# FFT filter and gated feed-forward on one core: an early table, an inverse in natural order, turns by halves

## The chip, the cores and the metric

The kernel runs on one core of one Trainium2 chip. Times are microseconds (us) of the device for one execution. The engines are PE (matmuls; its weight loads are listed apart as PEld), DVE, ACT and POOL (elementwise work), and SP, which here only issues transfers. Each has its own queue and works it off in order; they wait for each other by semaphores. The time before is the median of three runs: 863.05 us (862.38 to 863.38).

## The reference: what is computed

Eight batches of 3008 rows by 256 columns are filtered along the rows in the frequency domain, and every row of the result goes through a gated feed-forward:

```python
X = np.fft.rfft(x, axis=1)
Y = X * (filt_r + 1j * filt_i)[None]
y = np.fft.irfft(Y, n=x.shape[1], axis=1)          # (8, 3008, 256)
t = y.reshape(8 * 3008, 256)
gate = np.maximum(t @ w_gate, 0.0)                 # 256 -> 1536
out = (gate * (t @ w_val)) @ w_out                 # 1536 -> 256
```

Inputs and output are float32. All 24064 rows of the output are written.

## The kernel before

3008 is 94 times 32, so the transform is done in two steps, of 94 points over n1 and of 32 points over n2, each as matmuls with tables of cosines and sines. d is the column index, 0 to 255. For one batch the stages are these.

- Stage A (`a_bank`, L272, and for part of batch 1 `a_halves`, L329): matmul of rows of x with a table, `WA` or `WH`, results in PSUM tiles psA. ACT copies them to bfloat16.
- A turn: a transpose in blocks of 32 by 32 on DVE, which brings n2 to the partitions.
- The 32-point step (`fwd`, L442), the product with the filter (`product`, L459 to L462), the inverse 32-point step (`inv`, L485) into PSUM tiles psD. ACT and DVE copy these out (L498 for batch 0).
- Another turn, for batch 0 `turn_d`, from the tile AS0 (seen as `DS0`) to the tile dCb (seen as `D0`). Later batches go through a scratch area in HBM instead.
- Stage C (`item_c`, L605): matmul with `M1` for some columns n2 and one half h of d, into psY. ACT or DVE copies it to `yT`, in which d lies on the partitions (L613).
- Feed-forward: `gv` (L622: psV and psG; L625: ACT copies psV; L627: DVE makes prod) and `o_part` (L643, psO), in 47 blocks of 512 rows, 12 steps each.

The program has no scheduler: each engine gets its instructions in the order in which the Python code runs. The work of batches 1 to 7 up to stage C is placed among the feed-forward steps by hand (`at_step`). Ahead of the first feed-forward step stands a prologue: batch 0 from load to its first stage C, and much of batch 1's stage A. Its tiles come from a pool `pro`, which is closed at the end, so that the feed-forward's tiles take its place.

The end of the prologue goes like this. SP's queue loads batch 1's x: two quarters of the first half tile, six transfers of `load_halves` (rows n1 and n1 + 47 side by side), the last quarters, and then the table WH. `first_b` runs batch 0's 32-point steps with items of batch 1's stage A between (`item`). POOL adds and subtracts the two halves (`fold_halves`, L318 and L319). Then come, in this order, `turn_d` for both h (DVE), three items (PE), `a_halves` for both h (PE; needs WH and POOL's results), two items, stage C of batch 0's first two items, two more items, the first turn of batch 1, and on POOL a change of sign in every second row of the filter's imaginary part, `Fti` (L743). `conj` is a bfloat16 part of the tile `tabs`; `conj32` is its float32 copy, used in the prologue.

`y_items(0)` is 2: the first stage C has an item of five columns n2 and one of a single column, for each h. That makes twelve matmuls, each with a weight load of 128 by 128 from dCb.

In the kernel before, batch 0's inverse is laid down in pairs: `DS0` and `D0` are seen as (k, c, f) with c = 0 to 127, and f = 0 to 3 holding two columns n2 and, within each, the two halves h of d side by side. A turn moves 4-byte words, each the two halves of one (n2, c); the innermost two words of its access pattern lie side by side. `turn_d(h)` then covers the columns c of one half of c, and both halves h of d in each.

Of the kernel before, what the change touches and what calls it, by code (L numbers as in the profile page):

```python
# [12 lines left out]
FP32 = mybir.dt.float32  # L13
BF16 = mybir.dt.bfloat16
ALU = mybir.AluOpType
# [20 lines left out]
def _ap(t, offset_elems, ap_list):  # L36
    return dataclasses.replace(
        t, offset=t.offset + offset_elems, ap=[list(p) for p in ap_list]
    )
# [77 lines left out]
def kernel(  # L117
# [10 lines left out]
    nc = tc.nc  # L128
    B, S_, D = x.shape
# [11 lines left out]
    wh_h = np.zeros_like(wa_h)  # L141
# [5 lines left out]
    consts = ctx.enter_context(tc.tile_pool(name="consts", bufs=1))  # L147
# [5 lines left out]
    def bank(name, *shape):  # L153

        i = free.pop(0)
        t = ps.tile([128, *shape], FP32, tag=f"bank{i}", bufs=1, name=name)
        held[id(t)] = i, t
        return t

    def done(t):  # L160
        free.append(held.pop(id(t))[0])

    prologue = ExitStack()
    pro = prologue.enter_context(tc.tile_pool(name="pro", bufs=1))
# [6 lines left out]
    WA = pro.tile([128, 128], FP32)  # L171
    WH = pro.tile([128, 128], FP32)
    AS0 = pro.tile([128, 4, N2 // 2, D // 8, 4], BF16)
    DS0 = AS0.rearrange("p q n c f -> p (q n c f)").rearrange("p (k c f) -> p k c f", c=D // 2, f=4)
    dCb = consts.tile([128, 48, D], BF16)
    D0 = dCb[:, 0:32, :].rearrange("p n d -> p (n d)").rearrange("p (k c f) -> p k c f", c=D // 2, f=4)
    AS1 = [dCb[:, 32:48, :].rearrange("p n d -> p (n d)").rearrange("p (l c d) -> p l c d", l=NC2, d=D // 2)]
    WF = consts.tile([128, 4, 32], FP32)
    M1 = consts.tile([128, 2, N1], BF16)
# [4 lines left out]
    Fti = consts.tile([128, NG // 2, D], BF16)  # L184
# [7 lines left out]
    def load_x(b, engs, cols, ms=range(3)):  # L192
        w = NX2 * D
        for c, c0, c1 in cols:
            for m in ms:
                rows = min(32, B * N1 - (b * N1 + 32 * m))
                engs[m % len(engs)].dma_start(XF[c][m:m + 4 * rows - 3:4, c0:c1],  # L197
                              _ap(x, (b * N1 + 32 * m) * N2 * D + c * w + c0,
                                  [[N2 * D, rows], [1, c1 - c0]]))
# [2 lines left out]
    H = NG // 2  # L202
    FILT = ((filt_r, Ftr), (filt_i, Fti))
    tabs = pro.tile([128, tab_h.shape[1]], BF16, tag="tabs", bufs=1)
    conj32 = pro.tile([128, 2], FP32, tag="conj32", bufs=1)
    perm, conj, own = tabs[:, 0:64], tabs[:, 64:66], tabs[96:, 66:578]

    def make_back_t(r):
# [97 lines left out]
    def load_halves(b):  # L306

        for m in range(3):
            for s in range(2):
                r = 64 * s + m  # L310
                nc.sync.dma_start(halves[r:r + 61:4].rearrange("p k n d -> p k (n d)"),
                                  _ap(x, ((b * N1 + 16 * m) * N2 + NC2 * P_HALF + 4 * s) * D,
                                      [[N2 * D, 16], [N1 // 2 * N2 * D, 2], [1, 4 * D]]))
# [25 lines left out]
    def turn_pairs(dst, src):  # L339

        nc.vector.transpose(dst.bitcast(FP32).rearrange("p k c g -> p c k g"),
                            src.bitcast(FP32).rearrange("p n c g -> p c n g"))
# [5 lines left out]
    def turn_1(i):  # L348
        w = D // 8
        src = AS1[1 + i // 2].rearrange("p l c d -> p (l c) d")  # L350
        turn_a(ats[1][:, 1, :, i * w:i * w + w], src[:, :, i % 2 * w:i % 2 * w + w])
# [4 lines left out]

    def turn_d(h):

        e = slice(h * D // 4, h * D // 4 + D // 4)
        turn_pairs(D0[:, :, e], DS0[:, :, e])  # L360

    def store_half(b):
        w = N2 * D // 2
# [4 lines left out]
    def load_half(b):  # L368
        w = N2 * D // 2
        for q in range(4):  # L370
            nc.sync.dma_start(ats[b][32 * q:32 * q + 32, 0, 0:NG, :],
                              _ap(Abuf[b], q * NG * w, [[D // 2, 32], [w, NG], [1, D // 2]]))
# [102 lines left out]
    def inv(b, q):  # L475

        psD = [bank("psD", 2, D) for c in range(4)]
        last = 0 if b else 1
        for m in range(2):
            for k in range(last + 1):  # L480
                for r in range(2):
                    for c in range(4):
                        for e in range(2):
                            i = 2 * q + m
                            nc.tensor.matmul(psD[c][64 * e:64 * e + 64, m],  # L485
                                             (I2t, I2u)[k][32 * c:32 * c + 32, r, 2 * i + e, :],
                                             tus[b, i, e, k][32 * c:32 * c + 32, r],
                                             start=(k == r == 0), stop=(k == last and r == 1),
                                             tile_position=(32 * c, 64 * e))
        dst = sb.tile([128, 8, D], BF16, tag="dsb", bufs=3, name="dsb") if b else DS0  # L490
        def out(cs):
            for c in cs:
                copy = nc.vector.tensor_copy if (c % 2 if b else (q, c) in ((1, 2), (1, 3), (2, 0), (2, 1))) else nc.scalar.copy
                if b:
                    copy(dst[:, c:8:4, :], psD[c])
                else:
                    k, g = 4 * q + c // 2, c % 2 * 2
                    copy(dst[:, k:k + 3:2, :, g:g + 2], psD[c].rearrange("p m (f e) -> p m e f", f=2))  # L498
                done(psD[c])
        if not b:  # L500
            return out(range(4))

        def rest():
            out((2, 3))
            for z in range(4):
                nc.sync.dma_start(_ap(Dbuf[b], (64 * (z // 2) + z % 2) * NG * D + 8 * q * D,
                                      [[2 * NG * D, 32], [1, 8 * D]]),
                                  dst[32 * z:32 * z + 32])
        out((0, 1))
        return rest  # L510

# [38 lines left out]
    def d_rows(b, n2, h):  # L550

        if b:
            return dCs[b, n2 // 8][:, n2 % 8, h * 128:(h + 1) * 128]
        return D0[:, n2 // 2, :, n2 % 2 * 2 + h]

    def load_d(b):

# [34 lines left out]
    def y_items(k):  # L592

        n = 0
        while n < len(Y_COLS) and (Y_COLS[n][0] * N2 + Y_COLS[n][1]) * N1 < (k + 1) * W:
            n += 1
        return n

    def item_c(m, h):

        b, n2, c = Y_COLS[m]
        psY = bank("psY", c * N1)
        t = (b * N2 + n2) * N1
        for o, _, col, n1, w in runs(t, c * N1):
            nc.tensor.matmul(psY[:, o:o + w], d_rows(b, col, h),  # L605
                             M1[:, 1, n1:n1 + w] if b == 0 else M1[:NROW, 0, n1:n1 + w],
                             start=True, stop=True)
        o = 0
        while o < c * N1:
            p = (t + o) % NYT  # L610
            w = min(c * N1 - o, NYT - p)
            copy = nc.vector.tensor_copy if h and m < y_items(0) else nc.scalar.copy
            copy(yT[:, h, p:p + w], psY[:, o:o + w])  # L613
            o += w
        done(psY)
# [63 lines left out]
    q = NX2 * D // 4  # L679
# [32 lines left out]
    nc.sync.dma_start(hold, Ftr[0:2, 4, 0:8])  # L712
    load_x(1, sp, ((0, 0, 2 * q), (0, 2 * q, 4 * q)))
    load_halves(1)
    load_x(1, sp, ((1, 2 * q, 4 * q),))
    nc.sync.dma_start(WH, nc.inline_tensor(wh_h, name="dft_wh").ap())
    items = iter([(p, s, h) for p in (0, 1, 3) for h in range(2) for s in range(2)])

    def item(n):
# [9 lines left out]
    for h in range(2):  # L729
        turn_d(h)  # L730
# [4 lines left out]
    new_at(1)  # L735
    store_half(1)
    load_half(1)
    for m in range(y_items(0)):
        for h in range(2):
            item_c(m, h)  # L740
    item(2)
    turn_1(0)
    nc.gpsimd.tensor_scalar(Fti, Fti, conj[:, 0:1], 1.0, op0=ALU.mult, op1=ALU.mult)  # L743
    nc.sync.dma_start(WF, nc.inline_tensor(fold_h, name="dft_fold").ap())
    prologue.close()
    fs = ctx.enter_context(tc.tile_pool(name="fs", bufs=2))
# [87 lines left out]
```

## Time and profile before

| what | value |
|---|---|
| median of three runs | 863.05 us |
| the profiled execution, its own time | 863.78 us |
| its span, first to last instruction | 861.7 us |
| instructions | 20276 |
| PE busy | 845.9 us, 98% of the span |
| DVE busy | 578.5 us, 67% |
| ACT busy | 498.8 us, 58% |
| POOL busy | 462.0 us, 54% |
| mean granted TensorE clock | 0.999 |
| DMA | 101.66 MB, mean 118 GB/s |

A line of a group names source line, engine, operation, tiles (out <- in) and shape, then the count, after the bar the busy time and the mean of one in ns, and after the second bar how long the engine was idle just before and what ended that. A line of the order of time gives start, length, engine, source line, operation, tiles and count; instructions that follow each other are merged, so the length is that of the merged run. The chain is followed back from the last instruction: at each step to what released it, or to the instruction before it on its engine. Matmuls overlap in the array, so a start tells more than a length.

### The profile page before, as it was taken

To read this page: it belongs to the slowest core of one execution; us is meant where nothing else is said; L and a number is where in the kernel's file an instruction comes from. 1 tells how busy PE (TensorE), PEld (TensorE's weight loads), DVE (VectorE), ACT (ScalarE), POOL (GpSimd) and SP (SyncE) were. 2 spreads that over 40 slices of the span, in tenths; PEclk is the share of its full clock that TensorE was granted. 3 is DMA by queue.
4 is the path that set the end of the run, shared out by engine and by line. 5 is a ranking of instruction groups with operands and counts; after the bars stand their busy time and mean duration, and the time that the engine had idled before them with its cause. 6 is when DMAs were issued, how large, how long until landed. Compare 5 with 4: busy or idle time off the path is not lost.

```text
span 861.7 us, 20276 instructions
## 1 busy us (share of the span) xinstructions
PE 845.9 (98%) x7505; PEld 497.0 (58%) x7622; DVE 578.5 (67%) x865; ACT 498.8 (58%) x943; POOL 462.0 (54%) x496
## 2 busy tenths in 40 slices
PE   8899999999999999999999999999999999999998
PEld 4456655655555565655556565566655665666665
DVE  3878865777557776577765777658766578655553
ACT  5766565556655565555665565655566555565553
POOL 6847890488977765866757766767550032100001
PEclk9999999999999999999999999999999999999999
DMA  9995375333872339633295333853455222511112
GB/s 239 221 186 132 100 153 147 103 112 103 196 194 80 77 95 182 181 87 97 78 212 156 99 97 92 194 155 80 100 116 124 97 61 52 128 38 32 37 32 56
DMA packets 103150, 101.66 MB, mean 118 GB/s; under 512 B 21767, under 2 KB 90151, under 8 KB 102379
## 3 DMA queue, kind: packets, MB, share of 16 engines
q1 hardware_dynamic: 83695, 77.99, 34.6%
q0 software_dynamic: 18848, 21.68, 12.2%
q8 instruction: 60, 0.98, 0.5%
q10 hardware_dynamic: 508, 0.68, 0.3%
q14 instruction: 39, 0.32, 0.1%
HBM read 58.30 MB, written 45.88 MB: 121 GB/s over the span
## 4 chain that ended last, share of the span: by engine, by line
PE 92%; DMA 2%; DVE 2%; ACT 1%; SPq 1%; issue 1%
PE psG L622 29%; PE psO L643 28%; PE psV L622 25%; PE psF L408 3%; PE psY L605 2%; DVE prod L627 2%; PE psA L272 2%; ACT vsb L625 1%; PE psD L485 1%; DMA XF<-in_x_dram 1%; PE psX L442 1%; SPq L197 1%; DMA WH<-dft_wh 1%; DVE tt L462 0%; PE psA L329 0%
## 5 line engine op out<-in xcount | busy, mean ns | idle before, releaser
L627 DVE SCALAR_TENSOR_TENSOR prod<-psG,vsb 128x512 bf16<-128x512 f32 x564 | 389.0, 690 | 234.5 <-ACT vsb L625 229.6
L625 ACT CAST vsb<-psV 128x512 bf16<-128x512 f32 x564 | 331.9, 588 | 218.0 <-DVE prod L627 130.1
L622 PE MATMUL psG<-yT,WgT 128*128 128x512 bf16 x1118 | 333.1, 379 | 5.6
L643 PE MATMUL psO<-WoT,prod 128*128 128x256 bf16 x2256 | 336.5, 273 | 0.4
L622 PE MATMUL psV<-yT,WvT 128*128 128x512 bf16 x1023 | 313.6, 380 | 0.1
L643 PEld LDWEIGHTS <-prod 128*128 128x128 bf16 x2256 | 220.7, 98 | 143.4
L622 PEld LDWEIGHTS <-WgT 128*128 128x128 bf16 x1128 | 110.0, 98 | 133.8 <-issue 1.0
L472 POOL TENSOR_TENSOR pp<-tt,uu 128x256 bf16<-128x256 f32 x84 | 60.9, 725 | 170.5 <-DVE uu L462 160.6
L622 PEld LDWEIGHTS <-WvT 128*128 128x128 bf16 x1128 | 100.4, 98 | 36.9 <-issue 25.6
L613 ACT CAST yT<-psY 128x470 bf16<-128x470 f32 (+16 forms) x134 | 58.7, 456 | 46.8 <-PE psY L605 46.6
L652 ACT COPY osb<-psO 128x512 f32<-128x512 f32 x92 | 53.8, 585 | 25.3 <-PE psO L643 23.9
L665 POOL DMA_DIRECT2D out_dram<-osb x5 | 2.6, 535 | 119.2 <-ACT osb L652 117.7
L462 DVE TENSOR_TENSOR tt<-psX,Ftr 128x512 f32<-128x512 f32 (+1 forms) x93 | 63.3, 682 | 0.5 <-PE psX L442 0.5
L462 DVE TENSOR_TENSOR uu<-psX,Fti 128x512 f32<-128x512 f32 (+1 forms) x93 | 63.1, 680 | 0.6 <-DMA Fti<-in_filt_i_dram 0.6
L473 POOL TENSOR_TENSOR pp<-tt,uu 128x256 bf16<-128x256 f32 x84 | 60.9, 725 | 0.0
L394 POOL TENSOR_TENSOR fold<-XF 128x1024 f32<-128x1024 f32 x24 | 56.4, 2348 | 7.7 <-DMA XF<-in_x_dram 7.2
L395 POOL TENSOR_TENSOR XF<-XF 128x1024 f32<-128x1024 f32 x24 | 56.4, 2352 | 1.9
L381 POOL DMA_DIRECT2D XF<-in_x_dram x76 | 45.5, 601 | 2.0 <-issue 0.8
L264 POOL CAST scr<-prod 128x8 f32<-128x8 bf16 x19 | 3.6, 190 | 77.9 <-DVE prod L627 68.8
L415 DVE CAST asb<-psF 128x512 bf16<-128x512 f32 x48 | 30.9, 685 | 17.8 <-PE psF L408 17.8
L415 ACT CAST asb<-psF 128x512 bf16<-128x512 f32 x48 | 25.8, 589 | 28.9 <-PE psF L408 28.9
L605 PE MATMUL psY<-M,dCb 96*128 96x94 bf16 (+2 forms) x514 | 39.9, 205 | 0.0
(74 smaller groups left out, 460.7 us busy)
## 6 DMA issues: line engine op xcount, KB each, us to landing
Dbuf<-dsb SPq DMA_DIRECT2D x84, 128.0 KB
dCb<-Dbuf SPq DMA_DIRECT2D x56, 192.0 KB
XF<-in_x_dram POOLq DMA_DIRECT2D x38, 256.0 KB, 6.9
Abuf<-asb SPq DMA_DIRECT2D x96, 96.0 KB
at<-Abuf SPq DMA_DIRECT2D x18, 512.0 KB
XF<-in_x_dram POOLq DMA_DIRECT2D x76, 96.0 KB, 5.3
XF<-in_x_dram SPq DMA_DIRECT2D x28, 256.0 KB
out_dram<-osb SPq DMA_DIRECT2D x69, 94.0 KB
```

The lines of the kernel that those rows point to most:

```text
L394: tt(t, xp[:, 0:2], xp[:, 2:4], op=ALU.add)
L395: tt(xp[:, 2:4], xp[:, 0:2], xp[:, 2:4], op=ALU.subtract)
L415: copy(asf[:, :, q, :], banks[q])
L462: nc.vector.tensor_tensor(p, psX, filt, op=ALU.mult)
L472: nc.gpsimd.tensor_tensor(p[:, 0], tt[:, 0], uu[:, 1], op=ALU.subtract)
L473: nc.gpsimd.tensor_tensor(p[:, 1], tt[:, 1], uu[:, 0], op=ALU.add)
L605: nc.tensor.matmul(psY[:, o:o + w], d_rows(b, col, h), M1[:, 1, n1:n1 + w] if b == 0 else M1[:NROW, 0, n1:n1 + w], start=True, stop=True)
L613: copy(yT[:, h, p:p + w], psY[:, o:o + w])
L622: nc.tensor.matmul(pt[:, :W], w[:, h, ft * 128:(ft + 1) * 128], yT[:, h, y0:y0 + W], start=(h == 0), stop=(h == 1))
L625: nc.scalar.copy(vsb, psV[:, :W])
L627: nc.vector.scalar_tensor_tensor(prod, in0=psG[:, :W], scalar=0.0, in1=vsb, op0=ALU.max, op1=ALU.mult)
L643: nc.tensor.matmul(psO[:, t % 2], prods[ft][:, t * 128:(t + 1) * 128], WoT[:, ft, :], start=(ft == 0), stop=(ft == NFT - 1))
```

## The change

Three things are changed; the matmuls, their number and the order of the stages stay.

- The load of WH is issued on SP's queue after the six transfers of the halves and ahead of the last three transfers of x.
- Batch 0's inverse is laid down as rows of 256 columns d, one row for each n2. The copies out of psD write whole rows; `turn_d(h)` takes the columns of one half h of d, for all 32 rows, as 4-byte words of two neighbouring columns; the weight loads of batch 0's stage C read 128 neighbouring elements. The first stage C is done for the first half of d and then for the second.
- `conj32` lives in the pool that is not closed, and the change of sign of Fti takes its factor from there.

```diff
-    DS0 = AS0.rearrange("p q n c f -> p (q n c f)").rearrange("p (k c f) -> p k c f", c=D // 2, f=4)
+    DS0 = AS0.rearrange("p q n c f -> p (q n c f)").rearrange("p (j d) -> p j d", d=D)
     dCb = consts.tile([128, 48, D], BF16)
-    D0 = dCb[:, 0:32, :].rearrange("p n d -> p (n d)").rearrange("p (k c f) -> p k c f", c=D // 2, f=4)
+    D0 = dCb[:, 0:32, :]
...
-    conj32 = pro.tile([128, 2], FP32, tag="conj32", bufs=1)
+    conj32 = consts.tile([128, 2], FP32)
...
     def turn_d(h):
 
-        e = slice(h * D // 4, h * D // 4 + D // 4)
-        turn_pairs(D0[:, :, e], DS0[:, :, e])
+        dst, src = (t[:, :, h * D // 2:(h + 1) * D // 2].bitcast(FP32).rearrange("p n c -> p c n") for t in (D0, DS0))
+        nc.vector.transpose(dst, src)
...
-                    k, g = 4 * q + c // 2, c % 2 * 2
-                    copy(dst[:, k:k + 3:2, :, g:g + 2], psD[c].rearrange("p m (f e) -> p m e f", f=2))
+                    copy(dst[:, 8 * q + c:8 * q + c + 5:4, :], psD[c])
...
-        return D0[:, n2 // 2, :, n2 % 2 * 2 + h]
+        return D0[:, n2, h * 128:(h + 1) * 128]
...
     load_halves(1)
+    nc.sync.dma_start(WH, nc.inline_tensor(wh_h, name="dft_wh").ap())
     load_x(1, sp, ((1, 2 * q, 4 * q),))
-    nc.sync.dma_start(WH, nc.inline_tensor(wh_h, name="dft_wh").ap())
...
-    for m in range(y_items(0)):
-        for h in range(2):
+    for h in range(2):
+        for m in range(y_items(0)):
             item_c(m, h)
     item(2)
     turn_1(0)
-    nc.gpsimd.tensor_scalar(Fti, Fti, conj[:, 0:1], 1.0, op0=ALU.mult, op1=ALU.mult)
+    nc.gpsimd.tensor_scalar(Fti, Fti, conj32[:, 0:1], 1.0, op0=ALU.mult, op1=ALU.mult)
```

## The prediction

> **What bounds the kernel now.** I read the page's busy times first, then the chain that ended last, then that chain between 25 and 50 us, then the order of time of DVE, PE and POOL around 40 us, and last the groups kept apart by shape.
>
> ```profile
> PE 845.9 (98%) x7505; PEld 497.0 (58%) x7622; DVE 578.5 (67%) x865; ACT 498.8 (58%) x943; POOL 462.0 (54%) x496
> PE 92%; DMA 2%; DVE 2%; ACT 1%; SPq 1%; issue 1%
> ```
>
> PE carries the chain nearly all the time. After about 46.5 us, where the feed-forward matmuls (L622, L643) begin, the change touches nothing that PE waits for, so whatever it moves up to there is passed on to the end one for one. The chain there:
>
> ```profile
> 32.65 7.40 DMA WH<-dft_wh
> 40.05 0.14 issue
> 40.18 2.26 PE psA L329 x16
> 42.44 1.91 PE psA L272 x4
> 44.35 0.52 PE psY L605 x12
> 44.87 1.78 PE psA L272 x4
> 46.66 0.43 PE psV L622 x2
> ```
>
> PE waits for the table WH until 40.05 us. From there it runs without a gap: the matmuls of the halves, two items of batch 1, batch 0's first stage C (psY, twelve matmuls), two more items, feed-forward. The turns are not in this chain; they lie beside it:
>
> ```profile
> 35.98 2.84 PE L272 MATMUL psA<-XF,WA 128*128 128x512 f32 x6
> 36.29 2.37 POOL L319 TENSOR_TENSOR XF<-XF 128x1024 f32<-128x1024 f32 x1
> 37.47 4.70 DVE L341 STREAM_TRANSPOSE dCb<-AS 128x2048 f32<-128x2048 f32 x2
> 40.18 0.65 PE L329 MATMUL psA<-sum,WH 64*64 64x512 f32 x2 [1.35 <-DMA WH<-dft_wh]
> 44.19 0.68 PE L605 MATMUL psY<-M,dCb 128*128 128x94 bf16 x12
> ```
>
> DVE ends the two turns at 42.17 us and PE begins to read their result at 44.19: they have 2.0 us to spare. What one costs depends on its access pattern, and the kernel has both kinds:
>
> ```profile
> L341 DVE STREAM_TRANSPOSE dCb<-AS 128x2048 f32<-128x2048 f32 x2 | 4.7, 2383 | 0.1
> L341 DVE STREAM_TRANSPOSE at<-AS 128x1024 f32<-128x1024 f32 x4 | 4.7, 1225 | 13.1 <-ACT AS L284 13.1
> L336 DVE STREAM_TRANSPOSE at<-asb 128x512 f32<-128x512 f32 x4 | 4.3, 1082 | 1.5 <-ACT asb L296 1.5
> ```
>
> L341 walks pairs: two 4-byte words side by side, then a jump. It takes 2383/2048 = 1.16 and 1225/1024 = 1.20 ns per word. L336 walks single words, each a jump of 128 bytes on the reading side and 256 on the writing side from the last: 1082/512 = 2.11 ns per word, nearly twice as long.
>
> **The change part by part.**
>
> *Table of the halves.* WH goes on SP's queue ahead of the last three loads of x instead of behind them. SP is free to issue it at 30.22 us instead of 32.65; even with the same 7.40 us to landing that is 37.6, and with the queue in order it lands shortly after the halves, which POOL had at 33.87. PE ends the six matmuls before it at 38.82, and POOL's difference (L319), the third matmul's other need, ends at 38.66. So the wait of 1.35 us goes whole: PE would reach stage C at 44.35 - 1.35 = 43.0. The three loads that WH passes are issued one issue (0.6 us) later; their bytes and WH's are all in by about the 40.05 of before, and their first reader comes after the halves' 2.26 us, at about 41.1. Price nothing, 1 us of cover, and more below.
>
> *Natural order of d: copies out of psD.* The twelve copies (eight on ACT at 594 ns, four on DVE at 682) write rows without a break instead of pairs. The copies of the later batches write so from the same kind of bank: 593 on ACT, 685 on DVE. Zero.
>
> *Natural order: the turns.* Still two instructions of 2048 words, but their access pattern now takes the same 4-byte column of 32 rows, single words 512 bytes apart on both sides. That is L336's kind. The lower end of the unknown price is L341's 2.35 each (nothing here turns faster). From L336: its successor starts 0.98 us after it, so 4 x 0.98 = 3.92 as a step; with its whole duration, 4 x 1.08 = 4.32. The strides are longer than L336's, and if that doubled the price once more it would be 8.6, the upper end, for which no row speaks. I take 4.2 each, between the two readings of the nearest row and toward the dearer one. DVE starts them at 37.47 as before, since the copies cost the same: first done at 41.7, second at 45.9.
>
> The SBUF — State Buffer page of the Trainium skill (Specifications) says that SBUF has 16-byte lines and needs at least two accesses per line for full bandwidth. By that rule the new pattern loses what the pairs had, and the two rows above agree with it; a rule of one word per cycle whatever the stride would leave the turns at 2.35 and make the sum the first rival's below.
>
> *Stage C by halves of d.* The loop now does both items of the first half, then both of the second, so that the first half needs only the first turn. In the built order of the changed kernel, however, only the very first weight load waits for the first turn's count; the second weight load, still of the first half, already waits for the count of the second turn. Rows of the two halves interleave in one tile, so the waits do not tell them apart. PE is in order: one of the twelve matmuls can run at 43.0, eleven stand behind the second turn, and behind them the last two items and the whole feed-forward.
>
> So: second turn 45.87; first matmul after a wait 0.13 later (as after WH: 40.05 to 40.18), 46.0; eleven of the twelve, 11/12 x 0.52 = 0.48, to about 46.5, after which the next psA starts. Before, the first psY started at 44.19 and the next psA 0.52 later, 44.71. In starts: 46.0 + 0.48 = 46.5 against 44.71, **+1.8 us**. With 3.92 per turn the same sum gives +1.3, with 4.32 +2.1. The 1.35 us that WH saves is inside this: PE only waits longer, and without it nothing would be slower yet.
>
> What stands behind: DVE's copies of the second half into yT (0.81) come right after the matmuls and are covered by the 1.78 of psA, as before; the first turn of batch 1's at follows 1.8 later, and so does its reader, since PE is late as well. SP's store of the half for batch 1 waits for ACT copies ahead of stage C, which come earlier: no harm.
>
> *Weight loads of stage C.* Batch 0's 64 loads read rows without a break instead of every fourth element: 113 ns before, 98 in the later batches. They lie beside matmuls, whose starts are 0.52/12 = 43 ns apart in spite of 113-ns loads. Zero; the bound below is 64 x 15 ns = 1.0 us, which I do not expect.
>
> *Fti's signs.* The factor comes from a 4-byte copy that outlives the prologue. One POOL instruction, 2.86 us before (42.01 to 44.87), and POOL then idles 9.1 us; its reader comes at 63.7. Even at twice the time, nothing.
>
> **Against the runs shown.** The profiled execution took 863.78 with a span of 861.7, so 2.1 lies around the span; it is 0.7 above the median 863.05. The sum is made within the span and put on the median: 863.05 + 1.8 = 864.9, or 0.21%. A measurement of this kernel can tell about 0.2%, 1.7 us, from no change, so this sits at the border.
>
> **The rivals.**
>
> *The turns keep their pace (other side).* If single words cost what pairs do, the second turn ends at 42.17, ahead of PE's 43.0, and WH's gain stands: 863.05 - 1.35 = 861.7. It decides wherever both turns together take under 5.5 us. For: same opcode, same number of words. Against: L336. A turn that gains only partly lands between 861.7 and 864.
>
> *The granted clock falls in the gap.* PE would stand still from about 43.1 to 46.0, 2.9 us. The longest wait before is 1.35 us, and the granted clock stayed 1.00 there. But at the end of the run it does fall:
>
> ```profile
> 856.00:858.00 2.00, 1.90 (x18) 1.46 (x15) 0.49 (x2) 0.00 (x0) 1.76 (x4) 1.00 0.57 153
> 860.00:860.50 0.50, 0.00 (x0) 0.00 (x0) 0.00 (x0) 0.00 (x0) 0.00 (x0) 1.00 0.41 90
> 860.50:861.00 0.50, 0.00 (x0) 0.00 (x0) 0.00 (x0) 0.00 (x0) 0.00 (x0) 0.58 0.00 0
> 861.00:861.70 0.70, 0.00 (x0) 0.00 (x0) 0.00 (x0) 0.00 (x0) 0.00 (x0) 0.50 0.00 0
> ```
>
> (Busy time by stretch; the third value from the right is the granted clock.) It goes from 1.00 to 0.50 at about 860.6, 2.7 us after the last matmul's end at 857.9. A gap of 2.9 could meet that in some executions. PE at half speed for a time as long as the gap loses half of it, 1.5 us, twice that if two such times pass: 866.4 to 867.9. The page TensorE: Matmul & The Clock Gate of the Trainium skill (Part 1) gives a free-running window of about 3.4 us; by that page a gap of 2.9 would seldom fill one, and one window at half speed would cost 1.7.
>
> *The longer strides double the price again.* 8.6 per turn: second turn at 54.7, PE 8.8 us later than in the forecast: 873.7. Only the length of the strides speaks for it.
>
> **How the numbers follow.** The forecast's case, turns at L336's pace and no fall of the clock, 0.66: its own range is 864.0 to 865.4, and 0.36 of it lies over the 0.2% bound of 864.8, 0.30 under it. The clock falls: 0.17. Strides dearer still: 0.05. Turns at their old pace or partly: 0.12, of which 0.03 is faster by over 0.2% (weight loads or noise on top), 0.09 within. Slower 0.36 + 0.17 + 0.05 = 0.58, within 0.30 + 0.09 = 0.39, faster 0.03. The range reaches down a little below the forecast's own, 863.4, for partly slower turns, and up to 868.2, the end of the clock's case with some noise; the old pace and the doubled stride are left out.
>
> **What would show it.** The transposes of dCb at some 4.2 us each, ending near 46; PE waiting for WH no more, its halves from 38.9; one psY matmul near 43.1, then PE idle 2.4 to 3 us with the transpose of dCb as the releaser, eleven more from 46; everything later by 1.3 to 2.1. Wrong if the transposes take 2.4 us each, if the second psY matmul runs ahead of the second turn, or if the granted clock between 46 and 50 us is not 1.00.

## The result and the profile after

| | before | changed |
|---|---|---|
| median | 862.86 us (862.10 to 864.76, 6 runs) | 866.84 us (865.44 to 867.15, 6 runs) |
| profiled execution, its own time | 863.78 | 866.74 |
| its span | 861.7 | 864.6 |
| start of the feed-forward (first psV) | 46.49 | 49.45 |
| from there to the start of the last matmul | 811.14 | 811.11 |

The changed kernel is slower: ratio 1.0041, interval 1.0028 to 1.0054. (One of the executions further below, 1482.28 us long at a mean granted clock of 0.556, is left out of its kernel's figures.) The last two rows say where: all 2.96 us between the two profiled executions arise ahead of 49.45 us, and nothing is gained or lost behind it.

The page of the changed kernel, its busy times and the shares of the chain that ended last:

```profile
PE 847.4 (98%) x7505; PEld 496.8 (57%) x7622; DVE 582.1 (67%) x865; ACT 498.9 (58%) x943; POOL 462.1 (53%) x496
...
PE 92%; DVE 3%; ACT 2%; issue 1%; DMA 1%; SPq 0%; DVEq 0%
```

DVE is busy 3.6 us longer, and the chain that ended last now runs through it. The same chain from 37 us on (start, length, what):

```profile
37.33 8.34 DVE dCb L360 x2
45.71 1.04 PE psY L604 x11
46.76 2.85 PE psA L272 x4
```

The transfer of WH, which stood here before, is gone; the two turns stand in its place. In order of time (start, length, engine, line, operation, tiles, shape, count, idle time before it):

```profile
37.33 8.32 DVE L360 STREAM_TRANSPOSE dCb<-AS 128x2048 f32<-128x2048 f32 x2
...
38.62 0.65 PE L329 MATMUL psA<-sum,WH 64*64 64x512 f32 x2
...
42.32 0.20 PE L604 MATMUL psY<-M,dCb 128*128 128x94 bf16 x1
...
45.71 1.04 PE L604 MATMUL psY<-M,dCb 128*128 128x94 bf16 x11 [3.19 <-DVE dCb L360]
...
46.55 3.06 PE L272 MATMUL psA<-XF,WA 128*128 128x512 f32 x4
...
49.45 0.59 PE L621 MATMUL psV<-yT,WvT 128*128 128x512 bf16 x2
```

The halves start without a wait. PE does one psY matmul and then stands still for 3.19 us, until the second turn ends. The group of the turns (busy us, mean ns of one):

```profile
L360 DVE STREAM_TRANSPOSE dCb<-AS 128x2048 f32<-128x2048 f32 x2 | 8.3, 4220 | 0.1
```

4220/2048 = 2.06 ns per word. After the gap something more is lost: eleven psY that started every 43 ns before now take 0.84 us until the next psA starts, and the four psA that took 1.78 us from start to start take 49.45 - 46.55 = 2.90. The busy times by stretch give the reason (us; busy PE, PEld, DVE, ACT, POOL; granted clock; DMA share; GB/s):

```profile
44.00:46.00 2.00, 0.29 (x4) 0.29 (x5) 1.66 (x1) 0.00 (x0) 0.11 (x1) 0.84 1.10 162
46.00:48.00 2.00, 2.00 (x12) 1.36 (x10) 0.81 (x2) 0.69 (x2) 0.00 (x0) 0.50 1.31 245
48.00:50.00 2.00, 2.00 (x5) 0.73 (x5) 0.00 (x0) 1.00 (x4) 0.00 (x0) 0.80 1.07 310
```

The granted clock is 0.50 from 45.37 to 48.78 us by its records, 3.413 us, just as PE takes up work again. So the 2.96 us between the profiled executions are: eleven psY at 45.71 and, at full clock, the next psA at 45.71 + 0.48 = 46.19 against 44.71 before, +1.48; and half speed, (0.84 - 0.48) + (2.90 - 1.78) = +1.48.

The medians lie further apart, 3.98 us, because the profiled execution of before was 0.92 over its median and that of the changed kernel 0.10 under its own.

### The profile page after: what moved, and what is told of

Its sections match the earlier page's. It is cut to its first block, busy times and chain, and to the rows that moved or that the text cites. A ratio compares the mean times of both kernels' runs of the same rounds, so it can differ in the third digit from the quotient of the medians.

```text
span 864.6 us, 20275 instructions
## 1 busy us (share of the span) xinstructions
PE 847.4 (98%) x7505; PEld 496.8 (57%) x7622; DVE 582.1 (67%) x865; ACT 498.9 (58%) x943; POOL 462.1 (53%) x496
## 4 chain that ended last, share of the span: by engine, by line
PE 92%; DVE 3%; ACT 2%; issue 1%; DMA 1%; SPq 0%; DVEq 0%
PE psG L621 29%; PE psO L642 28%; PE psV L621 25%; PE psF L408 3%; PE psY L604 2%; PE psA L272 2%; DVE prod L626 2%; PE psD L485 2%; ACT vsb L624 1%; PE psX L442 1%; DVE dCb L360 1%; DMA XF<-in_x_dram 1%; SPq L197 0%; DVE tt L462 0%; ACT I2u L225 0%
```

## The experiments

Two theories stood against each other for each part of the loss: that the price of a turn sets the start of stage C and the fall of the clock comes on top; or that the slow part is the order of stage C, the table's move, or the feed-forward behind it.

### The table alone

The kernel before with only the early table:

```diff
     load_halves(1)
+    nc.sync.dma_start(WH, nc.inline_tensor(wh_h, name="dft_wh").ap())
     load_x(1, sp, ((1, 2 * q, 4 * q),))
-    nc.sync.dma_start(WH, nc.inline_tensor(wh_h, name="dft_wh").ap())
```

> The kernel before with the load of WH ahead of the last three loads of x, and nothing else: pairs, old order of stage C, old Fti. Theory (the early table is a gain that the slow turns bury): two turns of 2.35 us from 37.3 end at 42.0, PE reaches stage C at 42.3 as it did in the changed kernel, does not wait, and the granted clock stays 1.00; the time is 1.4 to 1.9 us under before, about 861.3. Rival (WH was never what PE had to wait for; something else, POOL's difference or the last x, takes its place): within 0.4 us of before.

Measured: 863.15 us (861.51 to 870.01, 12 runs) against 863.36 of before; ratio 1.0002, interval 0.9983 to 1.0022. A miss: the wait for WH is gone, but the median is only 0.21 us lower, which can't be told from none. Three of the twelve executions, 866.47 to 870.01, show a mean clock of 0.998 or less. The profiled execution happened to be the slowest, 870.01; there the feed-forward starts at 45.15, 1.34 ahead of before's 46.49, and the time is lost later. In order of time:

```profile
59.92 0.28 PE L442 MATMUL psX<-at,F 64*32 64x256 bf16 x1
65.04 1.05 PE L442 MATMUL psX<-at,F 64*32 64x256 bf16 x31 [4.83 <-DMA at<-Abuf]
```

That execution's busy times in three successive stretches of 3.41 us:

```profile
59.89:63.30 3.41, 0.31 (x2) 0.09 (x1) 0.58 (x1) 0.00 (x0) 1.90 (x3) 1.00 0.93 140
63.30:66.72 3.42, 1.68 (x33) 0.85 (x34) 0.69 (x1) 0.00 (x0) 0.70 (x1) 0.50 0.79 145
66.72:70.13 3.41, 3.41 (x11) 1.52 (x10) 1.29 (x2) 1.06 (x2) 0.73 (x2) 0.50 0.74 106
```

PE waits 4.83 us for `at`, batch 1's data on its way back from the scratch area, and then runs at half clock for two such stretches. It may be chance that this execution was the profiled one: in one comparison the 35 runs of the kernel before reached 868.37, there with a mean clock of 0.996. POOL's queue issues loads of batch 2's x from 53.16 us on, while that transfer is under way (SP issues it from 49.47 to 55.51). So the next kernel keeps the early table and puts all these loads on SP's queue, behind the transfer:

```diff
-                    if b == 2 and j > 1 or b == 3 and j > 0:
+                    if b == 2 or b == 3 and j > 0:
```

> The kernel before with the early table (as the first experiment), and batch 2's first two chunks of x loaded from SP's queue, behind the load of batch 1's at, instead of from POOL's queue beside it. The early table alone gave no gain in the median (863.15, single runs 861.5 to 870.0), and its profiled execution waited 4.8 us for the load of at. Theory (PE comes sooner to batch 1's 32-point step, and the load of at, shared with POOL's loads of x, is then late in many executions): with the other loads out of its way the wait goes, the runs draw together, median 861.3 to 861.8. Rival (the load of at is slow by itself, or the early table gains nothing): median near 863 and the spread stays.

Measured: 862.61 us (861.87 to 864.74, 11 runs) against 863.22; ratio 0.9995, interval 0.9986 to 1.0003. A miss again: a gain can't be told from none. No wait for `at` is left in the profiled execution, and the feed-forward starts at 44.10. The runs lie closer together than those of the early table alone, but so do the 23 of the kernel before beside them, 861.60 to 864.35, so that the one queue's part in it isn't shown. To part the two edits, the one queue was then run without the early table, beside the same with it.

> The kernel before with batch 2's first two loads of x on SP's queue instead of POOL's, its table of the halves still late. Theory (the wait for the table is a cost only in executions in which it lands late, about half a us in the median): the same median as the kernel before within 0.5 us, 862.7 to 863.7, and the run beside it with the early table as well 0.3 to 0.8 lower. Rival (the one queue brings the gain, the early table none): this kernel at 862.6 as the other.

> The kernel before with the early table and batch 2's first two loads of x on SP's queue, once more, beside the same without the early table. Theory: 862.6, and 0.3 to 0.8 below the run without the early table. Rival (the one queue brings the gain): no difference between the two.

Measured, against 863.37 of before: 863.02 us (862.42 to 864.98, 12 runs) without the early table, ratio 0.9995, interval 0.9983 to 1.0008; 862.56 with it (862.19 to 864.32, 11 runs), ratio 0.9990, interval 0.9980 to 1.0001. The early table is worth 0.46 us between the medians, within the expected 0.3 to 0.8; but the two intervals overlap, so it can't be told from none. In the profiled executions it is worth more: the feed-forward starts at 44.71 with it and at 45.93 without. The order of time of the kernel with the late table:

```profile
39.62 0.65 PE L329 MATMUL psA<-sum,WH 64*64 64x512 f32 x2 [1.32 <-DMA WH<-dft_wh]
```

That execution took 863.69, 0.67 over its median. The wait for the late table is not the same from execution to execution: 1.35 us in before's profile, 1.32 here, 0.58 in the Fti run below (862.94), 0.15 in the run that follows. The two longest are from executions above their medians. So it is a wait of an unlucky execution more than of the median; how long it is in the median one was not seen.

The changed kernel with the table put back behind the last loads of x:

> The changed kernel with the load of WH back behind the last x. Theory (the early table lengthens PE's gap to 3.2 us, and the granted clock falls because of that length): PE reaches stage C at 44.2, waits for the second turn until 45.7 or 45.8, a gap of about 1.4 us, which the kernel before also had without a fall; granted clock 1.00 throughout, time 1.3 to 1.6 above before, about 864.3, so some 2.4 us faster than the changed kernel although its table comes later. Rival (the clock falls for another reason, or the early table gains 1.9 us as in the kernel before): as the changed kernel, 866.8, or slower.

Measured: 865.57 us (864.75 to 868.84, 12 runs); ratio 1.0033, interval 1.0020 to 1.0046. Its waits of PE (us, times, longest) in the profiled execution:

```profile
PE psY L604 <- DVE dCb L360: 2.7, 1, 2.7
...
PE psA L329 <- DMA WH<-dft_wh: 0.2, 1, 0.2
```

A miss: the expected gap of 1.4 needed WH to be 1.35 late; it was 0.2 late, and the gap is 2.7. Seven runs lie at 864.75 to 865.71 with a mean clock of 1.00, five at 866.80 to 868.84 with 0.998 or less: the same two heights as in the changed kernel, whose one run at full clock took 865.44.

### The price of a turn

Two kernels each keep pairs on one side only. In the first, the kernel before with the early table, the copies write rows, and the turn reads single words (a column, 512 bytes apart) and writes pairs:

```diff
...
-        turn_pairs(D0[:, :, e], DS0[:, :, e])
+        src = DS0[:, :, e].rearrange("p n c f -> p n (c f)").bitcast(FP32)
+        nc.vector.transpose(D0[:, :, e].bitcast(FP32).rearrange("p k c g -> p c k g"),
+                            src.rearrange("p (k g) c -> p c k g", g=2))
...
```

> The kernel before with the early table, but the copies out of psD write rows (32 of them, each word the two halves of one column) so that the turns read single words 512 bytes apart; they still write pairs. Theory as far as it goes: a turn takes 2.35 us where both sides are pairs and 4.22 where neither is; which side it is that costs was not seen. If reading costs, 4.2 each and the time is that of the changed kernel, about 866.8; if writing costs, 2.35 each and 861.3; if each side costs half, 3.3 each, second turn at 43.9, and about 862.9. I lean to reading or to each alone being enough (4.2), since a stream runs no faster than its slower side.

In the second, the changed kernel, the copies write pairs, and the turn reads pairs and writes single words:

```diff
...
-        dst, src = (t[:, :, h * D // 2:(h + 1) * D // 2].bitcast(FP32).rearrange("p n c -> p c n") for t in (D0, DS0))
+        dst = D0[:, :, h * D // 2:(h + 1) * D // 2].bitcast(FP32).rearrange("p (k g) c -> p c k g", g=2)
+        src = DS0[:, :, h * D // 4:(h + 1) * D // 4].rearrange("p k c g e -> p k c (g e)").bitcast(FP32).rearrange("p k c g -> p c k g")
...
```

> The changed kernel with the copies out of psD writing pairs (two rows n2 side by side for every word of two columns), so that the turns read pairs and write single words 512 bytes apart; early table and halves stay. With single words read and pairs written a turn took 3.74 us, with single words on both sides 4.22, with pairs on both 2.35. If the slower side sets the pace and reading is it: 2.4 to 2.8 us, second turn before 43, no wait at stage C, 861.5 to 863 with the load of at as the next wait. If writing single words costs by itself: 3.5 to 4.2 and 865.5 to 866.8. I expect something near 3.7, both sides paying alike, since the sum of the two extra costs (1.4 and 0.5) otherwise leaves writing almost free.

Measured: 865.99 us (864.04 to 866.62, 12 runs), ratio 1.0021, interval 1.0009 to 1.0034; and 865.84 us (863.80 to 868.74, 12 runs), ratio 1.0029, interval 1.0019 to 1.0040. The groups of the turns, first that of writing pairs:

```profile
L361 DVE STREAM_TRANSPOSE dCb<-AS 128x2048 f32<-128x2048 f32 x2 | 7.4, 3742 | 0.1
```

and that of reading pairs:

```profile
L361 DVE STREAM_TRANSPOSE dCb<-AS 128x2048 f32<-128x2048 f32 x2 | 7.3, 3734 | 0.1
```

| ns per turn of 2048 words | write pairs | write single words |
|---|---|---|
| read pairs | 2383 (before) | 3734 |
| read single words | 3742 | 4220 (changed) |

Either side alone costs 1.35 us a turn, three quarters of what both cost. It doesn't matter which. Nor does the slower side alone set the pace: with single words on both sides a turn takes 0.48 us more than with them on one. The waits of PE in the kernel that reads pairs follow:

```profile
PE psY L606 <- DVE dCb L361: 2.2, 1, 2.2
```

With turns 0.49 us shorter, two of them bring the second psY matmul from 45.71 to 44.70, and the gap from 3.2 to 2.2. So the gap goes with the price of the turns. Yet the clock still fell in the profiled execution, and in these two kernels runs at full clock (864.0 to 864.8 and 863.8 to 864.6, four each) stand beside eight slower ones each.

### The clock in the gap

The changed kernel with twelve matmuls whose results are thrown away ahead of stage C:

```diff
+    warm(12)
     for h in range(2):
         for m in range(y_items(0)):
             item_c(m, h)
```

> The changed kernel with twelve matmuls of 512 columns on the prologue's tile junk, whose result nobody reads, ahead of batch 0's first stage C: 12 x 0.216 = 2.6 us of PE work in the gap of 3.2. Theory (the fall of the clock costs 1.5 us of the 4.0): granted clock 1.00 in every run, the eleven matmuls of stage C start at 45.7 as before, the next psA at 46.2 instead of 46.55 and the feed-forward 1.5 us earlier; 865.3. Rival (PE at half clock is hidden by another wait): 866.8 as the changed kernel, or slower by what the added matmuls take.

Measured: 865.37 us (865.02 to 866.01, 12 runs); ratio 1.0023, interval 1.0012 to 1.0033. In order of time:

```profile
42.59 2.75 PE L675 MATMUL psJ<-junk 128*128 128x512 bf16 x12
...
46.07 0.64 PE L604 MATMUL psY<-M,dCb 128*128 128x94 bf16 x11 [0.68 <-DVE dCb L360]
46.54 1.95 PE L272 MATMUL psA<-XF,WA 128*128 128x512 f32 x4
48.33 0.59 PE L621 MATMUL psV<-yT,WvT 128*128 128x512 bf16 x2
```

PE does more work, the second turn ends even 0.35 us later, and yet the median is 866.84 - 865.37 = 1.47 us lower than the changed kernel's: the eleven psY take 0.47 and the psA 1.79 again, and the mean clock is 0.999 or 1.00 in all twelve runs. The time is the expected one, the order of time only in part: because of the later turn the feed-forward starts 1.12 us earlier than in the changed kernel, and not 1.5. The two medians are also from different comparisons, in which the kernel before took 862.86 and 863.36; counted from there, the loss falls from 3.98 to 2.01, by 1.97. Within the changed kernel's own six executions, the one at full clock lies 1.49 below the median of the five others. So some 1.5 to 2 us of the loss is the fall of the clock, and the rest, 2.0 to 2.6 us by these runs, stays when the clock stays.

Real work can fill the gap as well. The changed kernel with the two items that follow stage C ahead of it:

```diff
+    item(2)
     for h in range(2):
         for m in range(y_items(0)):
             item_c(m, h)
-    item(2)
```

> The changed kernel with the two items of batch 1 that follow its first stage C moved ahead of it: real work fills part of the gap, where an earlier run put matmuls that are thrown away. Theory (the turns at 4.2 us set the start of stage C, the gap costs by itself and by the clock that falls in it): PE runs the two items from 42.3 to about 44.1, waits some 1.5 us for the second turn, all twelve psY stand at about 45.7 and the feed-forward begins about 47.0 to 47.3, since the copies into yT (0.8 us) are now uncovered. The clock stays at 1.00 in nearly all executions. Time 864.0 to 864.7, some 0.8 below the run with the thrown-away matmuls (865.37) and 2.3 below the changed kernel (866.84). Rival (what follows stage C is bound by something else, so that the order is worth nothing but the clock): feed-forward at 48.3 as there, time 865.4.

Measured: 864.56 us (863.99 to 866.16, 12 runs) against 863.37; ratio 1.0015, interval 1.0004 to 1.0027. In order of time:

```profile
40.29 3.70 PE L272 MATMUL psA<-XF,WA 128*128 128x512 f32 x8
43.83 0.21 PE L604 MATMUL psY<-M,dCb 128*128 128x94 bf16 x1
45.63 0.64 PE L604 MATMUL psY<-M,dCb 128*128 128x94 bf16 x11 [1.60 <-DVE dCb L360]
46.76 0.75 PE L621 MATMUL psV<-yT,WvT 128*128 128x512 bf16 x2 [0.49 <-ACT yT L612]
```

A hit in the median. The feed-forward starts at 46.76, 2.7 us sooner than in the changed kernel, and only 0.27 after before's, although the turns are as slow as ever (4385 and 4274 ns); the copies into yT are now in the way by 0.49. The clock did not stay in nearly all executions, though: seven runs lie at 863.99 to 864.63, and five at 865.41 to 866.16 with a mean clock of 0.998 or less, so that 1.60 and 0.49 us of waiting close together are still enough at times. This order is the best of the versions with slow turns.

When does the clock fall? Its records change only in steps of 3.413 us from the first record, at a phase that differs from execution to execution. Cut at those steps, the busy share of PE in the step just before a fall, and some of the lowest shares that were not followed by one, come out like this (worked out from the trace's matmuls and clock records):

| step before (us) | execution | PE busy | clock after it |
|---|---|---|---|
| 59.89 to 63.30 | early table alone | 0.09 | fell |
| 42.28 to 45.69 | stage C by items (below) | 0.11 | fell |
| 41.95 to 45.37 | changed | 0.17 | fell |
| 42.72 to 46.14 | reading pairs | 0.42 | fell |
| 43.82 to 47.23 | halves of d apart (below) | 0.42 | fell |
| 858.51 to 861.92 | reading pairs, its end | 0.45 | stayed |
| 43.38 to 46.79 | writing pairs | 0.48 | stayed |
| 43.64 to 47.05 | table late again | 0.53 | stayed |

So a step need not be idle: in these traces 42% busy was followed by a fall, twice, and 45% was not. The ends of matmuls in a trace are modelled, so the shares are not exact and the limit between the two isn't a sharp one. By these values some 0.57 x 3.413 = 1.95 us of idle time within one step does it. A gap of 3.19 us that falls anywhere against the steps holds 1.95 us in one of them unless a step ends between 1.24 and 1.95 us into it, which leaves out 0.71/3.413 = 21%: about 4 in 5 executions, and it was 5 of 6. For the gap of 2.7 us with the late table the same working gives about 6 in 10, and it was 5 of 12; for gaps of 2.2 and 2.3 us about half, and it was 8 of 12 each; for 0.68, none, and it was none. So this estimate agrees with the counts only roughly. A count here is of executions with a mean clock of 0.998 or less, and doesn't say where the clock fell: the kernel before, which has no such gap in its trace, shows it in 14 of 93 executions.

The page TensorE: Matmul & The Clock Gate of the Trainium skill (Part 1) gives a free-running window of 3413 ns; the length and the wandering phase agree with the records here. It has the fall come after an idle window, and there the runs differ: a window 42% busy was followed by one.

### The halves of stage C

The changed kernel with the old order of the loop:

```diff
-    for h in range(2):
-        for m in range(y_items(0)):
+    for m in range(y_items(0)):
+        for h in range(2):
             item_c(m, h)
```

> The changed kernel with the first stage C by items again (both halves of the five-column item, then both of the single column). Theory (the halves' order is worth nothing, because the second weight load waits for the second turn in either order): within 0.3 us of the changed kernel, 866.8, with the fall of the clock in most runs. Rival (the order lets PE do the first half in the gap): 0.2 to 0.5 us slower and a longer gap.

Measured: 867.99 us (866.82 to 869.29, 5 runs) against 863.22; ratio 1.0052, interval 1.0040 to 1.0064, which overlaps that of the changed kernel. In order of time:

```profile
42.44 0.20 PE L604 MATMUL psY<-M,dCb 128*128 128x94 bf16 x1
45.82 1.04 PE L604 MATMUL psY<-M,dCb 128*128 128x94 bf16 x11 [3.18 <-DVE dCb L360]
```

One matmul ahead of the gap and eleven behind it, as in the changed kernel, and everything 0.1 to 0.2 us later: the loop by halves brings nothing to this gap, because all but one of the first half's matmuls wait for the second turn. The median misses the expected 866.8: two executions, the profiled one among them, lie at 866.82 and 866.95, and three at 867.99 to 869.29 with a mean clock of 0.996, so that the clock stayed down longer there. None of those three is the profiled one, so the cause stays open.

To see what it could bring, dCb was laid down with the two halves of d apart, and the two items put between the halves of stage C. In that kernel part of batch 0's inverse is overwritten by batch 1's loads before it is read, so what follows stage C isn't the same work.

```diff
-    D0 = dCb[:, 0:32, :]
+    D0 = dCb[:, 0:32, :].rearrange("p n d -> p (n d)").rearrange("p (h n c) -> p h n c", h=2, c=D // 2)
...
-        return D0[:, n2, h * 128:(h + 1) * 128]
+        return D0[:, h, n2, :]
...
             item_c(m, h)
-    item(2)
+        if not h:
+            item(2)
```

> The changed kernel with the two halves of d in separate parts of the tile, so that the first half of stage C waits for the first turn alone, and with the two items that follow stage C done between its halves: the same work, in PE's gap. Theory: first half at 42.3, items from 42.6 to 44.4, second half after the second turn at 45.7 (a gap of 1.3 us), its copies into yT end at about 47.0, feed-forward from then; granted clock 1.00; 1.0 us better than the gap filled with idle work (865.4), so about 864.4, still above before. Rival (the halves wait for each other all the same, or the clock falls): 865.4 to 866.8.

Measured: 876.07 us (875.72 to 877.51, 5 runs), which says nothing, since waits of another kind come up after 47 us. Its beginning can be read, in order of time:

```profile
42.25 0.41 PE L605 MATMUL psY<-M,dCb 128*128 128x94 bf16 x6
42.50 1.95 PE L272 MATMUL psA<-XF,WA 128*128 128x512 f32 x4
45.78 0.43 PE L605 MATMUL psY<-M,dCb 128*128 128x94 bf16 x6 [1.33 <-DVE dCb L361]
```

All six matmuls of the first half run while the second turn is still at work. That the interleaved rows made the first half wait for both turns is shown; what the repair would bring as a whole stays open.

### The signs of Fti alone

```diff
-    conj32 = pro.tile([128, 2], FP32, tag="conj32", bufs=1)
+    conj32 = consts.tile([128, 2], FP32)
...
-    nc.gpsimd.tensor_scalar(Fti, Fti, conj[:, 0:1], 1.0, op0=ALU.mult, op1=ALU.mult)
+    nc.gpsimd.tensor_scalar(Fti, Fti, conj32[:, 0:1], 1.0, op0=ALU.mult, op1=ALU.mult)
```

> The kernel before with the change of sign of Fti alone: its factor from the four-byte copy that outlives the prologue. Theory (nothing waits for that instruction: POOL idles 9 us behind it): the same as before within 0.3 us, the instruction at 2.85 us. Rival (the four-byte copy in the lasting pool moves other tiles, and something of the feed-forward with them): a difference of 0.5 us or more, with the feed-forward's own length no longer 811.1 us from its first start to the last matmul's start.

Measured: 863.08 us (862.02 to 866.17, 12 runs) against 863.37; ratio 1.0004, interval 0.9992 to 1.0015. From the start of the feed-forward (45.62) to the last matmul (856.76) it takes 811.14, as before. The instruction on POOL takes 2863 ns, and 2862 before: no difference there, and none that can be measured in the time.

## Why the prediction was right, and where it was not

The forecast was 864.9, slower by 0.2%; it came out at 866.84, slower by 0.41%. The direction and its mechanism held, the likeliest case did not: 866.84 lies above that case's own 864.0 to 865.4, and within the whole range, 863.4 to 868.2, only because that reached up to the end of a rival's. What happened in five of six executions is that rival, in which the granted clock falls, given 0.17 and 866.4 to 867.9. One of the prediction's own signs of being wrong came true: the granted clock between 46 and 50 us was not 1.00, but 0.50 until 48.78.

- **The turns.** Taken at 4.2 us from L336's kind; they took 4.22 on the mean. L336's strides of 128 and 256 bytes and 512 here gave 2.11 and 2.06 ns per word: between these the length of the stride made no difference. (The sums for 3.92 and 4.32 us a turn come to +1.2 and +2.0, not +1.3 and +2.1.) The prediction took "pairs" and "single words" as two kinds; the runs show that single words on either side alone already cost most of it. The page SBUF — State Buffer of the Trainium skill (Specifications) asks for two accesses per 16-byte line; the four durations agree in direction, reading and writing alike.
- **The wait.** First psY near 43.1 and the rest at 46.0 were forecast, with a gap of 2.9; measured were 42.32, 45.71 and 3.19. One and eleven matmuls, as read from the built order. The next psA came at 46.55 where 46.5 was forecast, but by two errors that cancel: the turns ended 0.2 sooner, and the psY ran at half clock.
- **The clock.** This is the step that failed: "A gap of 2.9 could meet that in some executions." It weighed the gap by the only fall in the trace of before, 2.7 us behind the last matmul, and took a wholly idle stretch as the condition, which a gap of 2.9 could never give a step of 3.413. The runs show that about 1.95 us of idle time in a step is enough, which makes it the rule and not the exception for a gap of 3 us. The rival's price of 1.5 us came out, 1.48 in the trace, but partly by luck: it is half of the gap, and the clock stayed down for 3.413 us, whether the gap was 3.19 or, reading pairs, 2.17. In the changed kernel 0.34 of these 3.413 still lay in the gap, and half of the rest is near half of the gap. In the end of before's own trace the same condition could have been tested, since the step ahead of its last fall was 21% busy, not idle.
- **WH.** "The wait of 1.35 us goes whole" is right for the profiled execution. As a saving of the median it was too large: the early table brought 0.21 us between medians alone and 0.46 with the one queue, both within what can't be told from none. The prediction took the +1.8, which has those 1.35 in it, over to the median unchanged. At full clock the changed kernel took 865.44 once, and with the gap filled 865.37; over the kernel before beside each, that is 2.58 and 2.01 where 1.8 was forecast, which is in that direction. That WH is the reason is not shown.
- **What was priced at nothing.** The copies out of psD took 594 and 685 ns, as forecast; the weight loads are hidden; Fti's signs changed nothing. From the start of the feed-forward to the last matmul it is 811.1 to 811.3 us in every profiled execution in which the clock was full behind that start, so that whatever is lost ahead of it reaches the end one for one, as the prediction had it.

No version here beats the kernel before by more than can be told: the nearest is the early table with batch 2's loads on one queue, 0.9995 (0.9986 to 1.0003) and 0.9990 (0.9980 to 1.0001) in two comparisons.

## What to carry to other kernels

A transpose by 4-byte words is priced by both of its access patterns; keep at least two neighbouring words innermost on the reading and on the writing side, and don't give up one for the sake of tidy rows elsewhere. A gap on PE of over 2 us can cost more than itself, since the clock may fall for 3.4 us behind it; weigh such a gap by how much of it lies within one step, and put work that is ready ahead of the wait. And a wait that a profile shows for a transfer is the wait of that one execution: look at how far it stands from the median before counting on it as a gain.

## What the runs showed of the hardware

The granted clock fell after steps of 3.413 us in which PE was 42% busy (two executions), and held after one of 45%, by modelled ends of matmuls. In the early table's profiled execution it came back only after the second step: the first one at half clock was 49% busy, the second wholly. Single words on one side of a DVE transpose cost 1.83 ns per word, on both 2.06, pairs on both 1.16. And one and the same transfer, WH queued last, was issued at 31.49 to 32.65 us in four profiled executions and took 6.70 to 7.43 us to land where the chain shows it, so that PE waited 0.15, 0.58, 1.32 or 1.35 us for it.
